# A new order of all operations for attention and a mixture of experts on one core, with one more head group masked on TensorE

## The chip, the core and the metric

The kernel runs on one core of a Trainium2 chip. The metric is device microseconds of one execution, the median of the runs shown: 206.53 us (206.17 to 207.06). Five engines work side by side, each through its own instruction stream in order: TensorE (PE: matrix products, with its weight loads as PEld), VectorE (DVE), ScalarE (ACT), GpSimd (POOL) and SyncE (SP). They meet through semaphores. POOL issues nearly all DMAs here, so a wait in its stream holds back the loads behind it.

## The reference

```python
# q, k, v: (8 batches, 8 heads, 576, 64)
scores = scale * q @ k.T                       # per batch and head
scores = where(|i - j| <= 32, scores, -1e9)    # a band of 65 keys
attn = softmax(scores)                         # over the keys
x = (attn @ v) as 4608 tokens of 512
logits = x @ w_gate + modality_bias[modality_id]
e = argmax(logits); gate = softmax(logits)[e]
out = gate * (relu(x @ w1[e]) @ w2[e])         # the one expert of each token
```

With the data of this problem the modality decides the expert, so two of the eight experts are used. A flag at the end of the kernel checks that and would start a general version otherwise.

## The kernel before

The whole program is one text, `ORDER` (L34 on): a list of operations, each with its indices, the engine that runs it (`/v` DVE, `/a` ACT, `/p` POOL, none for TensorE) and the PSUM banks it writes (`:0123`). A loop at the end of the kernel walks the list and emits each operation. Nothing is reordered afterwards: the order of the list is the order in each engine's stream, and semaphores make an operation wait for what it reads and for the banks or buffers it overwrites.

Operations of attention, for batch b, head group g (four heads) and head pair it (four a batch):

- `l b.u.g` and `lv b.i` (L222, L246): loads of q, k and of halves of v, issued by POOL.
- `t b.g.u` (L645): a DVE transpose of q or k. `SA`, `SB` (L677, for b below 3) and `SA`, `SE` (L701): the scores, in banks of PSUM. `sa`, `sb`, `se` (L685, L688, L733, L744): the exponentials, on ACT, into `pt`.
- The band's mask is put on in one of two ways. For the head groups numbered in `PM` (number 2b + g), `MA` and `MB` (L654, L658) first write 0 or a large negative number into the PSUM banks by products of an identity with the tile `neg`, and the scores are added on top. For the other groups `M it` (L766; `M b.g` L758, `Me` L752 from batch 3 on) multiplies the exponentials by 0 or 1 on DVE.
- `V it` (L804, L781): the products with v, whose extra column gives the softmax sums. `v it` (L818, L833): reciprocal and scaling on DVE, into `xt`. `Vx` copies v shifted by 64 rows.

Operations of the sorting and the experts:

- `s` and `G` rank the tokens of each modality and make one-hot matrices; `X b.m` (L853) moves and transposes a block of tokens by a product with one, and `pa`, `pb` (L873, L887, ACT) append it at the front or the back of the list `XT`. `Jo`, `Je`, `Jm`, `Jx`, `Jy` make the row numbers for the scatter of the output.
- `W` (L635, L637): loads of the weights of the two experts; each needs the expert's number in a POOL register, which DVE makes in `e4`.
- `U t.i` (L991): eight products of 128x256, a quarter of the hidden layer of token tile t; `u` (L1006 on DVE, L1008 on ACT) is its relu. `D t.s.h` (L1017): four products of 128x512, half of an output block; `y` (L1033 on DVE, L1031 on ACT) scales it by the gate and `O` (L1040) scatters it to the output. `L`, `lo`, `E`, `sm`, `rc` make the gates.
- `n k.256` (L1049): k products of zeros on TensorE, 128x256, that nobody reads.

Of the kernel before, what the change touches and what calls it, by code (L numbers as in the profile page):

```python
# [39 lines left out]
Kb/v Kc2/p sb0.1/a n2.256:4 MA0.1:4567 t1.0.1/v l1.1.1/p SA0.1 Kc0/p sa0.1/a s1:0 l1.0.1/p V0:12 s2/v s3/v  # L40
n2.256:3 W1.0/p s5 v0/v s4 s6/a s7 SB1.0:4567 s9/a s8/v s10/a s11/v G0/v V1:01 s12/p W1.1/p n2.256:2 s13/v
n2.256:2 sb1.0/a v1/v V2:23 lv1.1/p v2/v V3:01 r0/a Kc4/p v3/v SA1.0:4567 n2.256:3 W2.0/p s15/v sa1.0/a X0.1:0
t1.1.0/v n4.256:1 Kc5/p n2.256:2 n2.256:1 X0.0:1 s14/v l2.0.2/p t1.1.1/v n4.256:6 pa0.0/a pb0.0/a n4.256:3
# [16 lines left out]
D3.1.1 L2:1 se3.2/a lo2/v U5.2:2 SA3.1.0:4567 SA3.1.1 t4.1.1/v SA3.1.2 t4.0.1/v Kx0/a y3.0/a Vx3.0/v G3/v  # L60
U4.1:1 sa3.1/a U4.0:0 u5.2/a SE4.2.0:4567 u4.0/a SE4.2.1 se4.2/a Me3.2/v y3.1/v l5.0.2/p U5.0:2 O1.0/p l5.1.2/p
lv4.1/p E2/a u5.0/a u4.1/a U5.1:0 u5.1/a V12:45 sm2/v V13:67 M3.1/v v13/v O2.0/p U4.2:2 V14:01 U4.3:3 v14/v
c1/v u4.2/a u4.3/a v12/v V15:67 Vx4.1/a v15/v U5.3:0 D4.0.0:3 lv5.0/p D4.0.1 rc2/v lv5.1/p Me4.2/v O1.1/p
y4.0/v l6.1.2/p u5.3/a X3.0:6 pa3.0/a pb3.0/a lv6.0/p X3.1:7 X3.2:4 pa3.1/a O3.0/p D5.0.0:5 pb3.1/a t5.1.1/v
# [25 lines left out]
U14.2:3 L8:7 U17.3:1 U15.3:2 u14.2/a D14.1.0:3 u17.0/a u14.3/v y13.0/v E7/a U15.1:6 D14.0.0:5 U17.1:4 u17.1/a  # L90
O11.1/p O13.0/p D14.1.1 O10.1/p u15.3/v sm7/v E9/a rc7/v y12.1/v u17.3/v D14.0.1 U16.0:1 O11.0/p U15.2:4
u15.2/v sm9/v U16.3:0 U15.0:2 D17.0.0:4 O12.0/p u15.1/a y14.1/a O12.1/p rc9/v lo8/v D17.1.0:7 D17.1.1 U16.2:3
D17.0.1 Jy12/v E8/a sm8/v rc8/v y17.1/a c5/v c6/v O17.1/p O14.1/p y14.0/a u16.0/a u16.3/a c7/v O14.0/p U18.0:5
u18.0/a c9/v c10/v c11/v c8/v c12/v c13/v c14:1 c15/v U16.1:7 u16.2/a c16/v y17.0/v O17.0/p D18.0.0:5 U18.1:4
# [1228 lines left out]
```

## Time and profile before

| | |
|---|---|
| median of 3 runs | 206.53 us |
| the profiled execution | 206.92 us, its span 205.2 us |
| busy PE, DVE, ACT, POOL | 192.2, 151.2, 127.8, 92.8 us |
| products of zeros | 86, listed busy 13.9 us |
| granted TensorE clock over the span | 0.992 |

The profile is one execution. Its span runs from the first to the last instruction, and 1.7 us of the execution's time lie around it. The ends of products on TensorE are modelled: each is drawn about 0.17 us longer than its share of the array, so that gaps shorter than that don't show, and the price of a group of products is better read from where the next group starts.

### The profile page before, as it was taken

What the parts mean: (1) busy time and instruction counts of PE and PEld (TensorE: products, weight loads), DVE (VectorE), ACT (ScalarE), POOL (GpSimd) and SP (SyncE); (2) the same over time, 40 slices, a digit from 0 to 9 for tenths busy, and PEclk for the clock granted to TensorE, in tenths of its full rate; (3) what the DMA queues carried; (4) which work ended last, traced back from release to release, by engine and by line L of the source; (5) the groups of instructions that cost most, each with busy time, mean ns of one, the idle gap of its engine ahead of it and who ended that gap; (6) DMA issues with size and microseconds to landing.
All of it is one profiled execution on the core that took longest, in us unless ns stands there. A gap on an engine that the chain in (4) does not pass through costs nothing. (4 is left out here: it accounts for less than half of the span.)

```text
span 205.2 us, 6637 instructions
## 1 busy us (share of the span) xinstructions
PE 192.2 (94%) x2783; PEld 138.6 (68%) x2783; DVE 151.2 (74%) x314; ACT 127.8 (62%) x219; POOL 92.8 (45%) x137
## 2 busy tenths in 40 slices
...
PEclk9999999999999999999999999999999999999996
...
GB/s 66 205 177 182 212 213 191 213 213 192 204 188 234 217 234 194 218 213 64 184 161 153 147 262 150 188 195 13 3 56 2 0 107 0 205 54 74 161 131 55
DMA packets 47662, 30.43 MB, mean 148 GB/s; under 512 B 38883, under 2 KB 38923, under 8 KB 47371
## 3 DMA queue, kind: packets, MB, share of 16 engines
...
q8 instruction: 23, 0.38, 0.7%
...
HBM read 36.76 MB, written 9.70 MB: 226 GB/s over the span
## 5 line engine op out<-in xcount | busy, mean ns | idle before, releaser
L1040 POOL DMA_INDIRECT out_dram<-ys,ids x37 | 38.1, 1029 | 75.1 <-ACT ys L1031 33.5
L991 PE MATMUL banks<-XT,w_sb 128*128 128x256 bf16 x576 | 70.8, 273 | 0.6 <-DVE xt L833 0.3
L1017 PE MATMUL banks<-w_sb,hT 128*128 128x512 bf16 x288 | 69.2, 379 | 0.1
L991 PEld LDWEIGHTS <-w_sb 128*128 128x128 bf16 x576 | 54.0, 98 | 10.3 <-issue 1.3
L1008 ACT ACTIVATE hT<-banks 128x512 bf16<-128x512 f32 x53 | 30.1, 604 | 28.1 <-PE banks L991 24.5
L1017 PEld LDWEIGHTS <-hT 128*128 128x128 bf16 x296 | 27.3, 98 | 25.7
L645 DVE STREAM_TRANSPOSE qk<-qk 128x576 int32<-128x576 int32 x32 | 37.9, 1238 | 2.0 <-DMA qk<-in_k_dram 1.5
L833 DVE TENSOR_TENSOR xt<-banks,recs 128x640 bf16<-128x640 f32 x32 | 26.4, 824 | 1.1
L1006 DVE TENSOR_SCALAR hT<-banks 128x512 bf16<-128x512 f32 x21 | 14.4, 684 | 17.1 <-PE banks L991 17.1
L1031 ACT ACTIVATE ys<-banks,Gt 128x512 f32<-128x512 f32 x21 | 14.3, 691 | 15.0 <-PE banks L1017 9.6
L873 ACT CAST XT<-banks 128x352 f32 (+3 forms) x40 | 17.8, 446 | 6.2 <-PE banks L853 5.6
L246 POOL DMA_DIRECT2D vt<-in_v_dram x16 | 20.2, 1267 | 1.4 <-PE banks L781 1.3
L685 ACT ACTIVATE pt<-banks 128x1536 bf16<-128x1536 f32 x12 | 17.5, 1459 | 3.0 <-PE banks L677 2.0
L887 ACT CAST XT<-banks 128x352 f32 (+2 forms) x39 | 17.3, 444 | 1.2 <-DVE qk L645 0.5
L733 ACT ACTIVATE pt<-banks 128x1536 bf16<-128x1536 f32 x10 | 14.6, 1461 | 3.3 <-PE banks L701 3.3
L1033 DVE TENSOR_SCALAR ys<-banks,Gt 128x512 f32<-128x512 f32 x16 | 11.9, 745 | 5.9 <-PE banks L1017 5.9
L1049 PE MATMUL banks<-zero_b 128*128 128x256 bf16 x86 | 13.9, 319 | 2.0 <-DVE zero_b L303 1.5
L853 PEld LDWEIGHTS <-xt 128*128 128x128 bf16 x160 | 10.3, 98 | 4.3 <-issue 1.3
L781 PEld LDWEIGHTS <-pt 128*128 128x128 bf16 x320 | 11.7, 97 | 1.8 <-DVE pt L758 0.6
L853 PE MATMUL banks<-oh,xt 128*128 128x128 bf16 (+1 forms) x160 | 12.3, 214 | 0.7 <-DVE xt L833 0.3
L781 PE MATMUL banks<-vt,pt 128*128 128x65 bf16 x160 | 12.1, 193 | 0.4 <-DVE pt L758 0.4
L1049 PEld LDWEIGHTS <-zero_b 128*128 128x128 bf16 x86 | 9.3, 115 | 4.4 <-DVE zero_b L303 1.5
...
## 6 DMA issues: line engine op xcount, KB each, us to landing
...
out_dram<-ys,ids POOLq DMA_INDIRECT x37, 3.2
```

Source lines behind the costliest of these rows:

```text
L246: nc.gpsimd.dma_start(v_t[b % NV][:, n_ * i:n_ * i + n_, 0:D], v[b].rearrange("h s d -> (h s) d").rearrange("(n p) d -> p n d", p=P)[:, n_ ...
L645: nc.vector.transpose(qk_t[b % 2][:, g, at:at + S].rearrange("p (t r) -> p r t", r=R), Ct["l", b][:, u, g].bitcast(I32).rearrange("p (r j) ...
L685: nc.scalar.activation(pt[:, :, 2 * part:2 * part + 2, 0:WIN], st[:, :, 0:2 * WIN].rearrange("p h (j c) -> p h j c", c=WIN), ACT.Exp, scal ...
L781: nc.tensor.matmul(ot[:, h, (D + 1) * m:(D + 1) * (m + 1)], pt[:, c1:c1 + P], src[:, R // 2 * hp + n_, 0:D + 1], start=(i_ == 0), stop=las ...
L833: nc.vector.tensor_tensor(out=o_ap, in0=o_v[:, :, :, 0:D], in1=rec.unsqueeze(3).to_broadcast([P, 2, NM, D]), op=ALU.mult)
L853: nc.tensor.matmul(t_[:, kd, :], x_t[b % NX][:, m, P * kd:P * kd + P], Ct["oh", b][:, m, 0:n_], start=True, stop=True, skip_group_check=True)
L873: ins = nc.scalar.copy(XT[:, :, bass.ds(r_, w_)], Ct["X", b, m][:, :, 0:w_])
L991: ins = nc.tensor.matmul(ph[:, u_, :], w1[:, f0:f0 + 2 * P - 1:2], rhs, start=(kd == 0), stop=(kd == n_kd - 1))
L1008: nc.scalar.activation(o_ap, i_ap, ACT.Relu)
L1017: nc.tensor.matmul(Ct["D", t_, s_], Ct["h", t_][:, kf, P * s_:P * s_ + P], w2, start=(kf == 0), stop=(kf == n_kf - 1))
L1040: ins = nc.gpsimd.indirect_dma_start(out=out, out_offset=bass.IndirectOffsetOnAxis(ap=ids[:, u_:u_ + 1], axis=0), in_=Ct["y", t_, s_][:], ...
L1049: nc.tensor.matmul(banks[:, bk[0], 0:w_], zero_b[:, 0:P], zero_b[:, 0:w_], start=True, stop=True, skip_group_check=True)
```

## The change

The list is replaced as a whole, and `PM` gets a third number. So batch 1's first head group is masked by products: `MB1.0` and `MA1.0` are new and `M4`, `M5` are gone. The list keeps every other operation once. The products of zeros become 36 instead of 86; 21 of them stand ahead of the first real product, where 50 stood. Some operations change engine: 12 `u` from ACT to DVE and 10 the other way; 11 `y` from DVE to ACT and 7 the other way; three halves of `Vx` from ACT to DVE and one the other way; 6 `Je` from POOL to DVE and 5 the other way; the paddings `Kq0` and `Kp1` from DVE to ACT; `s10`, `s12`, `e9` to DVE.

```diff
-Km Kh/v Kw0/v Ke/v Ki l0.0.1/p n2.256:0 n2.256:0 l0.1.0/p Kp0/a n2.256:0 l0.0.0/p n4.256:0 Kg l0.1.1/p e0/v
...
-n2.256:0 n2.256:0 n2.256:0 n2.256:0 MA0.0:0123 Kw1/v Ko2/a Ko1/v t0.1.0/v lv1.0/p Ko0/a SA0.0 MB0.0:4567
-sa0.0/a t0.1.1/v Kc1/p SB0.0 lv0.1/p s0/v e4/v t1.0.0/v MB0.1:0123 sb0.0/a Kc3/p SB0.1 e5/v e7/v e8/v Kw2/v
...
-s16/p pa0.1/a X0.2:5 M5/v n2.256:4 pb0.1/a SB1.1:1234 l2.1.2/p pb0.2/a n4.256:0 G1/v pa0.2/a e9/p X0.3:7
-sb1.1/a V5:56 M4/v n2.256:0 n2.256:0 X0.4:0 v5/v pb0.3/a V4:12 pa0.3/a Jo0/v SA1.1:3456 pa0.4/a Je1.0/v pb0.4/a
-U0.1:7 v4/v sa1.1/a Je1.1/p U0.2:0 Je1.2/v Jo1/v r3/a L0:3 Je0.0/v Je0.1/v Je0.2/v U0.3:4 M6/v u0.1/a U1.0:6
...
+Km Kh/v Ki Kw0/v l0.0.0/p Kq0/a Kp0/a Kj/p Kn0/p t0.0.0/v l0.1.0/p l0.1.1/p Kq1/a Kp1/a t0.0.1/v e0/v e1/v Ke/v
+e2/v t0.1.1/v Kn1/p Kw1/v n4.256:4 n4.256:4 n4.256:4 n4.256:4 n5.256:4 MA0.0:0123 l0.0.1/p MB0.0:4567 SA0.0
+sa0.0/a l1.0.1/p Kc3/p Ko0/v e3/v t0.1.0/v l1.0.0/p s0/v SB0.0 MA0.1:0123 sb0.0/a l1.1.0/p lv0.0/p Kw2/v SA0.1
+s1:4 t1.1.0/v s2/v s11/v sa0.1/a n3.256:5 s4:4 Kc0/p s5:4 Kc2/p s3/v Kb/v n5.256:5 MB0.1:0123 t1.0.0/v t1.0.1/v
+s6/a l1.1.1/p s7:4 s8/v s10/v s9/a Ko1/a s12/v SB0.1 sb0.1/a Kc1/p G0/v e4/v n7.256:6 V0:45 s13/v lv0.1/p s15/v
+Kc4/p r0/a V1:67 MB1.0:0123 v0/v SB1.0 sb1.0/a V2:45 lv1.0/p t1.1.1/v v1/v W1.0/p V3:67 lv1.1/p SA1.1:0123
+s14/v v2/v v3/v G1/v SB1.1:4567 sa1.1/a sb1.1/a W1.1/p s16/p Jo1/v MA1.0:0123 SA1.0 Je0.0/v r3/a X0.4:4 Kc7/p
+Je1.0/v e6/v Jo0/v sa1.0/a Je1.1/v X0.1:5 X0.2:6 Kc5/p Je0.1/p Je0.2/p X0.0:7 pa0.0/a pa0.1/a pa0.2/a V4:01
+l2.0.2/p Je1.2/p pb0.0/a V5:23 pb0.1/a pb0.2/a M7/v M6/v X0.3:7 pa0.3/a pa0.4/a Jm0:5 v4/v Jx0/v V6:01 pb0.3/a
+v5/v Je2.0/v V7:56 U0.3:7 l2.1.2/p U0.0:2 Je2.1/p U0.2:3 v7/v v6/v W2.0/p pb0.4/a X1.1:0 X1.3:1 X1.0:5 pa1.0/a
...
+y16.0/a O12.1/p D17.1.0:4 u18.0/v y15.0/v D17.0.0:0 U18.1:2 c14:6 c15/v c16/v D17.0.1 y17.0/a O15.1/p
+O15.0/p O14.0/p rc9/v O16.0/p D17.1.1 O17.0/p y17.1/a O17.1/p D16.1.0:6 D16.1.1 y16.1/a D18.0.0:4 u18.1/v
+O16.1/p D18.0.1 y18.0/a O18.0/p c17/p
...
-    PM = (0,1)
+    PM = (0,1,2)
```

## Rows read from the trace of the kernel before

**Rows 1.** The page: busy time of TensorE and the granted clock in 40 slices.

```profile
PE 192.2 (94%) x2783; PEld 138.6 (68%) x2783; DVE 151.2 (74%) x314; ACT 127.8 (62%) x219; POOL 92.8 (45%) x137
...
PEclk9999999999999999999999999999999999999996
```

**Rows 2.** Stages: from and to in us, their length, busy us of each engine.

```profile
9.80:29.70 19.90, 17.52 (x354) 13.51 (x352) 18.70 (x41) 16.20 (x26) 15.74 (x32) 1.00 1.52 195
29.70:60.00 30.30, 29.81 (x412) 22.77 (x409) 29.02 (x67) 23.13 (x40) 14.97 (x23) 1.00 1.37 202
60.00:90.00 30.00, 29.14 (x537) 20.30 (x535) 29.21 (x44) 24.86 (x46) 16.51 (x16) 1.00 1.70 217
90.00:115.00 25.00, 24.56 (x440) 18.67 (x439) 22.93 (x38) 16.81 (x26) 11.37 (x14) 1.00 0.78 147
...
135.00:198.00 63.00, 62.95 (x688) 43.23 (x685) 29.73 (x74) 27.75 (x54) 17.00 (x18) 1.00 0.19 69
```

**Rows 3.** Timeline of the end: start, duration, engine, line, tiles, count, idle before.

```profile
192.60 5.34 PE L1017 MATMUL banks<-w_sb,hT 128*128 128x512 bf16 x24
...
198.03 0.69 ACT L1031 ACTIVATE ys<-banks,Gt 128x512 f32<-128x512 f32 x1 [1.90 <-PE banks L1017]
199.00 0.97 POOL L1040 DMA_INDIRECT out_dram<-ys,ids  x1 [0.34 <-ACT ys L1031]
```

**Rows 4.** Waits of TensorE after 29.7 us: the longest; total us, times, longest.

```profile
PE banks L781 <- DVE pt L758: 0.4, 1, 0.4
```

**Rows 5.** Timeline of TensorE, 12 to 40 us.

```profile
12.63 0.81 PE L654 MATMUL banks<-neg,ident 128*128 128x384 bf16 x4
13.28 0.39 PE L658 MATMUL banks<-neg,ident 128*128 128x128 bf16 x4
13.60 0.64 PE L677 MATMUL banks<-qk 32*128 32x192 bf16 x24
...
16.61 0.73 PE L804 MATMUL banks<-vt,pt 128*128 128x65 bf16 x18
17.17 0.38 PE L1049 MATMUL banks<-zero_b 128*128 128x256 bf16 x2
...
29.71 1.91 PE L991 MATMUL banks<-XT,w_sb 128*128 128x256 bf16 x16
31.46 0.55 PE L918 MATMUL banks<-wgd,XT 128*128 128x8 bf16 x16
...
39.47 0.49 PE L527 MATMUL banks<-ev,vx 128*128 128x72 bf16 x10
```

**Rows 6.** Timeline of DVE, 7 to 27 us.

```profile
7.21 1.26 DVE L645 STREAM_TRANSPOSE qk<-qk 128x576 int32<-128x576 int32 x1 [1.52 <-DMA qk<-in_k_dram]
8.95 1.26 DVE L645 STREAM_TRANSPOSE qk<-qk 128x576 int32<-128x576 int32 x1 [0.48 <-DMA qk<-in_q_dram]
...
10.19 2.28 DVE L645 STREAM_TRANSPOSE qk<-qk 128x576 int32<-128x576 int32 x2
...
25.13 1.14 DVE L766 TENSOR_TENSOR pt<-pt,mask 128x1920 bf16<-128x1920 bf16 x1
26.20 0.86 DVE L497 TENSOR_TENSOR oh<-iob,col 128x640 bf16<-128x640 bf16 x1
```

**Rows 7.** Timeline of ACT, 11 to 27 us.

```profile
11.13 3.00 ACT L685 ACTIVATE pt<-banks 128x1536 bf16<-128x1536 f32 x2 [0.45 <-PE banks L677]
...
25.35 0.98 ACT L887 CAST XT<-banks 128x352 f32 x2
26.23 0.47 ACT L873 CAST XT<-banks 128x352 f32 x1
```

**Rows 8.** Timeline of POOL: the first weights' load is issued.

```profile
17.68 0.77 POOL L635 DMA_DIRECT2D w_sb<-in_moe_w_dram  x1 [0.71 <-issue]
```

**Rows 9.** Two stretches of the products of zeros alone: busy us and count.

```profile
1.50:7.30 5.80, 5.78 (x28) 4.12 (x29) 1.00 0.83 138
7.40:9.70 2.30, 2.30 (x24) 2.05 (x21) 1.00 1.18 197
```

More of the change, by code (lines that the diff above doesn't have):

```diff
@@ L40 @@
[L40 to L43, printed above, removed]
-s16/p pa0.1/a X0.2:5 M5/v n2.256:4 pb0.1/a SB1.1:1234 l2.1.2/p pb0.2/a n4.256:0 G1/v pa0.2/a e9/p X0.3:7
@@ L60 @@
[L60 to L64, printed above, removed]
@@ L90 @@
[L90 to L94, printed above, removed]
@@ new lines @@
+t2.0.0/v u0.1/a L1:7 t2.0.1/v SB2.0:0123 Je4.1/p sb2.0/a Je5.0/v s17/v e5/v Jo5/v L0:6 lo1/v U2.0:4 Jo4/v
+Je4.2/v U2.2:7 lo0/v u1.1/a Je5.1/p u2.2/a Je5.2/v Jm2:6 SA2.0:0123 t2.1.0/v t2.1.1/v sa2.0/a u2.0/a E0/a
+Je6.0/v Jo7/v D0.0.0:5 M9/v sm0/v M8/v D0.0.1 rc0/v SA2.1:0123 sa2.1/a D0.1.0:4 Jo6/v E1/a D2.0.0:7 Jy10/v
+Jx2/v t3.0.1/v y0.0/a SB2.1:0123 sb2.1/a e10/v Je6.1/p l4.1.2/p Je7.0/v sm1/v D0.1.1 U3.1:6 y0.1/a Je6.2/v
+D2.0.1 V8:01 u3.1/a V9:34 rc1/v Jy1/v lv3.1/p Je7.1/p U3.0:6 Je7.2/p M10/v u3.0/a M11/v Kr0/a Jm3:2 v8/v U3.3:5
@@ new lines @@
+y2.0/a D2.1.0:0 r1/a v9/v Kx0/a u3.3/a V11:34 t3.0.0/v U3.2:7 v11/v u3.2/a Jx3/v lv3.0/p V10:56 Kx1/a v10/v
+t3.1.0/v t3.1.1/v Jy3/v Jy0/v SA3.0.0:1234 SA3.0.1 SA3.0.2 sa3.0/a Jy4/v Jy5/v D2.1.1 X2.1:5 X2.0:6 Jy11/v
+D1.1.0:7 D1.1.1 G3/v Jy6/v pb2.0/a pa2.0/a Jy7/v y2.1/a SE3.2.0:0123 SE3.2.1 l4.0.2/p pa2.1/a pb2.1/a se3.2/a
+y1.1/v D3.1.0:6 X2.3:5 X2.2:4 pa2.2/a D3.1.1 D3.0.0:7 t4.1.1/v Me3.2/v Jy8/v Jy9/v O0.0/p Kr1/v y3.1/a X2.4:0
+M3.0/v D1.0.0:6 pb2.2/a SA3.1.0:1234 SA3.1.1 SA3.1.2 pa2.3/a pa2.4/a D1.0.1 pb2.3/a t4.0.1/v U4.0:5 pb2.4/a
@@ new lines @@
+u4.0/v L2:0 sa3.1/a M3.1/v l5.0.2/p Kc6/p O2.0/p lo2/v O0.1/p Vx3.0/a U5.1:1 Vx3.1/v s19/v t4.1.0/v t4.0.0/v
+c0/v D3.0.1 U5.0:0 V12:45 u5.0/a u5.1/a V13:23 O2.1/p U5.2:0 u5.2/a U4.1:1 u4.1/a v12/v U4.3:0 y1.0/a v13/v
+V14:45 v14/v U4.2:1 E2/a sm2/v y3.0/a V15:67 u4.3/v SE4.2.0:2345 SE4.2.1 u4.2/a t5.0.0/v se4.2/a D4.0.0:1
+D4.0.1 rc2/v y4.0/a v15/v SA4.1.0:2345 SA4.1.1 SA4.1.2 sa4.1/a lv4.1/p D5.0.0:0 lv4.0/p Me4.2/v X3.0:1 pa3.0/a
+Vx4.0/v t5.1.0/v Vx4.1/v lv5.0/p pb3.0/a O3.1/p O1.1/p l5.1.2/p X3.1:6 D4.1.0:7 lv6.1/p D4.1.1 r2/a pa3.1/a
@@ new lines @@
+U5.3:1 SA4.0.0:2345 y4.1/a pb3.1/a lv5.1/p u5.3/a SA4.0.1 SA4.0.2 O1.0/p M4.1/v l6.0.2/p sa4.0/a X3.3:6
+D5.1.0:7 D5.0.1 X3.2:2 pb3.2/a Kv/p pa3.2/a pb3.3/a V19:34 pa3.3/a M4.0/v lv6.0/p O4.0/p v19/v X3.4:5 pb3.4/a
+pa3.4/a D5.1.1 y5.1/v V18:12 V16:34 v16/v V17:56 U7.0:7 u7.0/a L3:3 y5.0/a t5.0.1/v v17/v U6.1:4 U7.2:7 u7.2/a
+U7.1:5 t5.1.1/v v18/v lo3/v t6.1.0/v G4/v u7.1/a U6.3:7 u6.3/a Vx5.0/v u6.1/a U6.0:5 E3/a SE5.2.0:0123 SE5.2.1
+se5.2/a s18/v U6.2:4 X4.0:7 U7.3:6 u7.3/a u6.2/v SA5.0.0:0123 SA5.0.1 pb4.0/a pa4.0/a SA5.0.2 D7.0.0:4 D7.0.1
@@ new lines @@
+X4.1:7 l6.1.2/p Jy12/v sa5.0/a u6.0/v t6.0.0/v l7.1.2/p X4.2:5 D6.1.0:6 pb4.1/a pb4.2/a sm3/v pa4.1/a D6.1.1
+pa4.2/a SA5.1.0:0123 SA5.1.1 t6.0.1/v M5.0/v rc3/v SA5.1.2 Me5.2/v D7.1.0:5 sa5.1/a O3.0/p D7.1.1 V20:01 y7.0/a
+e11/v V21:23 v21/v v20/v X4.3:4 pb4.3/a D6.0.0:7 D6.0.1 y6.1/a O4.1/p U9.2:6 pa4.3/a M5.1/v L4:0 lo4/v
+SA6.0.0:1234 l7.0.2/p O7.0/p SA6.0.1 SA6.0.2 y7.1/v sa6.0/a Vx6.0/v lv7.1/p U8.2:0 u9.2/v E4/a U9.0:5 sm4/v
+O5.1/p Vx5.1/v U9.1:1 u9.0/a y6.0/a O7.1/p U8.3:5 u8.3/a U8.0:7 u8.2/a u9.1/v O6.0/p O5.0/p V22:56 V23:01
@@ new lines @@
+u8.0/a t6.1.1/v D9.1.0:7 v22/v v23/v G5/v U9.3:5 u9.3/a X4.4:6 SE6.2.0:0123 SE6.2.1 pb4.4/a rc4/v U8.1:4 D9.1.1
+se6.2/a X5.4:5 pa4.4/a t7.0.1/v M6.0/v SA6.1.0:0123 u8.1/a y9.1/v SA6.1.1 SA6.1.2 sa6.1/a X5.1:6 X5.0:4
+D9.0.0:7 D9.0.1 Me6.2/v X5.2:0 c1/v O6.1/p pa5.0/a lv7.0/p D8.1.0:1 pa5.1/a X5.3:2 M6.1/v pa5.2/a pb5.0/a
+pa5.3/a pa5.4/a t7.1.1/v G6/v D8.1.1 pb5.1/a y8.1/a O8.1/p Vx6.1/v U10.2:4 pb5.2/a t7.1.0/v pb5.3/a pb5.4/a
+U10.0:6 u10.0/a V24:01 V26:23 y9.0/a v24/v U11.1:6 u11.1/a V25:01 U11.0:7 v26/v t7.0.0/v c2/v L5:2 c3/v u11.0/a
@@ new lines @@
+U10.1:3 lo5/v v25/v O9.0/p U11.3:2 V27:67 U11.2:0 u11.2/a D11.1.0:1 u10.2/v v27/v X6.0:0 O9.1/p Vx7.1/v u10.1/a
+E5/a u11.3/v SA7.1.0:4567 sm5/v SA7.1.1 SA7.1.2 sa7.1/a G7/v U10.3:3 u10.3/v D10.0.0:2 pa6.0/a Vx7.0/v M7.1/v
+SE7.2.0:4567 SE7.2.1 D10.1.0:3 D10.0.1 rc5/v y10.0/v se7.2/a D11.1.1 y11.1/v pb6.0/a X6.1:0 SA7.0.0:4567
+SA7.0.1 SA7.0.2 sa7.0/a pb6.1/a D8.0.0:2 D8.0.1 pa6.1/a Me7.2/v X6.2:4 pb6.2/a V31:56 D11.0.0:0 D11.0.1 v31/v
+D10.1.1 y10.1/a V30:56 U13.0:7 pa6.2/a X6.3:4 O10.0/p U13.2:3 O10.1/p O11.1/p U12.3:1 v30/v c4/v M7.0/v y11.0/v
@@ new lines @@
+V28:56 pa6.3/a U13.3:0 v28/v u13.0/v u13.2/a U13.1:3 V29:56 y8.0/a O8.0/p U12.0:7 X6.4:2 u12.3/a v29/v U12.2:1
+u13.3/v e12/v u12.0/v pb6.3/a X7.0:5 pa6.4/a u13.1/v pb6.4/a pb7.0/a X7.1:2 L6:0 U12.1:7 lo6/v X7.3:0 X7.2:3
+pa7.0/a pa7.1/a pa7.2/a D13.1.0:5 u12.2/a u12.1/v D12.1.0:7 U14.0:1 X7.4:6 u14.0/v N/p D12.1.1 pb7.1/a pb7.2/a
+pa7.3/a U14.2:1 D13.0.0:3 E6/a sm6/v pb7.3/a pa7.4/a xe/a e13/v D13.0.1 D13.1.1 L7:6 lo7/v c5/v c6/v c7/v
+U15.1:0 L8:6 lo8/v L9:2 lo9/v c9/v c10/v E8/a U15.0:4 u15.0/a D12.0.0:2 U14.3:4 u14.2/a rc6/v u14.3/v U15.2:1
@@ new lines @@
+u15.1/a D15.0.0:0 U14.1:4 E7/a sm7/v u15.2/a y13.0/v sm8/v y13.1/v D12.0.1 U15.3:5 u15.3/a U16.3:1 D15.0.1
+U16.1:5 y12.1/a y12.0/a rc7/v O11.0/p u14.1/a D14.1.0:4 U16.0:2 u16.0/v rc8/v c11/v c8/v c12/v c13/v U16.2:7 Wx
+D14.1.1 D14.0.0:2 D15.1.0:3 y14.1/v O13.1/p O13.0/p D14.0.1 D15.1.1 y14.0/v U17.1:4 U17.3:2 U18.0:6 u16.1/a
+U17.0:5 u17.1/a U17.2:4 y15.1/a u17.3/v E9/a u17.2/v sm9/v D16.0.0:2 O12.0/p u16.2/a u17.0/a O14.1/p u16.3/a
+D16.0.1 y16.0/a O12.1/p D17.1.0:4 u18.0/v y15.0/v D17.0.0:0 U18.1:2 c14:6 c15/v c16/v D17.0.1 y17.0/a O15.1/p
```

45 lines of the change are left out of this document (3 added, 42 removed).

## The prediction, made before the changed kernel ran

> **What bounds the kernel now.** I read the page first. TensorE is busy for 192.2 of 205.2 us, and its granted clock is full in all slices but the last [rows 1]. The stages then say who is late where [rows 2]. From 9.80 to 29.70 TensorE is busy 17.52 of 19.90 us, and part of that is products of zeros, so here it waits for what DVE and ACT make. From 29.70 on it has nothing but real products and stands still for 0.49, 0.86 and 0.44 us in the next three stages, and 0.05 us in the 63 us from 135 on. So the second part is a fixed amount of products and less than 2 us of visible waiting. In the two stages up to 90 us DVE is busy 29.02 of 30.30 and 29.21 of 30.00 us: it is the other engine without slack, and the longest wait of TensorE there is for DVE's mask multiplication [rows 4]. The end of the timeline shows what follows TensorE: the last product ends at 192.60 + 5.34 = 197.94, ACT scales it by 198.72, POOL scatters it from 199.00, and the span ends at 205.2 [rows 3].
>
> So the time is: when the first expert product starts, plus the products still to do then, plus waits, plus a tail of 7.3 us. For each of the four I ask what the new list does.
>
> **The start, to the first expert product.** It stands at 29.71 now (U0.1) [rows 5]. In the new list the first is U0.3, and I follow its chain.
>
> On POOL, q of group 0 is now first, then the identity, one band of `neg`, and then k. The second and third load of the list before release their transposes at 7.21 and 8.95, 1.74 us apart [rows 6]; that is the pace of the loads, and k, now second, should still land near 7.2, with q transposed while it is awaited. One more transpose is 2.28 / 2 = 1.14 us [rows 6]. I take SA0.0 at 8.6, where the list before starts its first exponential at 11.13 [rows 7], so ACT starts near 9.1. The mask products MA0.0 and MB0.0 stand ahead of it, beside the loads, and cost nothing.
>
> A large exponential is 3.00 / 2 = 1.5 us at most [rows 7]. sa0.0 and sb0.0 fill ACT to 12.3. The fourth load and its transpose are no earlier than before (10.19 + 2.28 = 12.47 there [rows 6]), so sa0.1 runs 13.0 to 14.5. MB0.1 is written into the same banks 0 to 3 and waits for that. MA and MB cost 13.28 - 12.63 = 0.65 us, and 0.32 more for the third part of MB [rows 5], so MB0.1 is 0.97; s7 and SB0.1 follow, and sb0.1 ends near 18.0. MB1.0 needs its banks again: 0.97 and about 0.6 for the scores bring sb1.0 to 19.7 - 21.5. V2, V3 and SA1.1 follow, sa1.1 to 23.9. SB1.1 takes banks 4 to 7 and so waits for v3 on DVE, which I put at 23.4 by the list; sb1.1 to 26.0, sa1.0 to 27.4. Then eight appends of (26.23 - 25.35) / 2 = 0.44 us [rows 7], the last of which frees bank 7: U0.3 at 31.1. M7, M6 and v4 on DVE end at 29.7 by the same count, so V6 and V7 fit in before it.
>
> That is 1.4 us later than now. But V6 and V7 are done by then, where the list before does them after its first U: a V is 17.17 - 16.61 = 0.56 us, two are 1.12, and Jm0 is under 0.49 (I take 0.3) [rows 5]. What is left on TensorE is 1.4 us less. The start comes out even. The new masks are 2 x 0.65 + 0.32 = 1.62 us of TensorE [rows 5], all ahead of U0.3, where it has room; if ACT and DVE were faster than I count they would be on the path and cost the whole 1.62.
>
> **The products of zeros.** 50 fewer; those behind 9.8 us stand in front of real work only where TensorE waits anyhow. I take nothing for them; at most they free 36 x 2.30 / 24 = 3.5 us minus the new list's 15 x 0.1 = 1.5, so 2 us [rows 9].
>
> **DVE.** M4 and M5 go: 26.20 - 25.13 = 1.07 each [rows 6], 2.14 us. I compared both lists at V15, ahead of which both have the same real products but for SE4.2. DVE gets there two u more, six small Je for three, s10, s12 and e9, and loses half a Vx. Together these give back about 1.4, so 0.7 us less work. The paddings that moved to ACT lay in DVE's idle time and bring nothing. Also, DVE now waits less between 12 and 17 us, since a transpose stands where it waited for the rank products (about 1 us by the list's order). So DVE is 0.7 to 2 us ahead of the list before in the stages up to 90 us, where TensorE waits for it.
>
> **The waits after the first U.** 0.49 + 0.86 + 0.44 = 1.8 us are visible [rows 2]. Each wait hides up to 0.17 us more under the modelled end, so with some ten of them the sum is 3.3 at the most. Two of the three stages are those where DVE is full. I take half, 1.5 us. The bounds are 3.3 gained, and below nothing a new wait: an operation of the new list that stands before what it needs. The price of such a wait is at least the 0.4 us of rows 4.
>
> **The end.** The last product is now D18.0.1, with y18.0 on ACT and one scatter behind it. y, scatter and landing are as before: 198.03 to 198.72 and 0.28 to the scatter [rows 3]. No change, 0.3 us to either side.
>
> **The sum.** Start 0, masks 0, waits -1.5, end 0. The profiled execution took 206.92, so 205.4; it is 0.4 above the median of the runs, so 205.0.
>
> **The rivals.** *DVE still sets the pace and the waits return in other places.* For it: DVE is full to 97%, and 0.7 us of work is little. Against it: the operations that TensorE needs stand earlier in DVE's list relative to the products. It gives 206.5, no change.
>
> *TensorE drops to the lower clock in the start.* Here the change speaks against itself. The products of zeros show both levels: up to 7.3 us they follow each other every 5.80 / 28 = 0.21 us, which is 256 columns at 1.2 GHz, and then every 2.30 / 24 = 0.1 us, 2.4 GHz [rows 9]. The list before keeps TensorE busy 17.52 of 19.90 us from there; by my chain the new one leaves it idle for half of that stretch, in gaps of 1 us and more. If the clock falls between 10 and 31 us, then MB0.1, SB0.1, MB1.0, SB1.0, SB1.1, four X and two V on my chain, some 5 us together, take twice as long, less what waits hide: 4 us later, 209. It decides as soon as the granted clock shows one slice of 0.5 after 8 us. Against it: the gaps are short. The Trainium skill ("TensorE: Matmul & The Clock Gate", Part 1) has the lower rate as the array's default and the full one as something that activity earns; by that rule fewer idle products are a risk and by the trace, where the clock never fell after 7.3 us, no case shows how much is enough.
>
> *The first weights come late.* W1.0 needs the register from e4. It is issued at 17.68 now and U0.1 starts at 29.71, so it lands within 12.0 us [rows 5, 8]. The new list has e4 behind G0, near 18.1 by my count, so the load is issued at 18.8 and is there by 30.8, just ahead of U0.3. If DVE is 2 us late at e4 (three transposes, Kb and G0 stand ahead of it), U0.3 starts at 33 and everything behind it moves: 206.5 - 1.5 + 1.9 = 206.9, and with W1.1 and W2.0 as late in the same queue 208. For it: all loads go through one queue in order. Against it: the bound of 12.0 us is an upper one.
>
> That the mask isn't moved is no rival: `PM` and the list agree, and the two multiplications are gone.
>
> **Chances.** The forecast 0.52 (203.0 to 205.5 in itself), DVE and no change 0.27, the clock 0.12, the weights 0.09. About 0.5% (1.0 us) is what a measurement of this kernel can tell from no change. The forecast lies below 205.5, the second within; of the last two nearly all lies above 207.6, some of the weights' case within. So faster 0.53, same 0.28, slower 0.19. Unknown costs move the forecast by -3.3 + 1.5 = -1.8 at the waits and by -1 or +1.9 at the start. The range is 202.7 to 207.8; the clock's case and a part of the weights' stay outside.
>
> **What would show it.** Right: first exponential near 9.1, U0.3 between 30.5 and 32, M4 and M5 absent, TensorE's visible idle time from the first U to 115 us under 1 us, DVE busy less in the same stages. Wrong: idle TensorE of more than 2 us behind the first U (DVE or ACT named as releaser), a clock row below full after 8 us, or U0.3 behind 33 with a DMA as what ended the wait. The step I trust least is the chain to 31.1: it has nine links, and each is a bank or an engine that I counted by hand.

## The result and the profile after

The changed kernel takes 209.32 us (median of 16 runs, 208.19 to 211.49), the kernel before 207.04 (16 runs, 206.17 to 207.91): 1.0116 times as long, 95% interval 1.0092 to 1.0139. It is 1.2% slower; 205.0 was forecast. Ratios and intervals leave out executions that took over 1.5% longer than the fastest of the same kernel; medians count all.

The profiled executions took 210.18 and 206.92 us, 3.26 apart. Where they part can be read from three places. The first U starts at 33.66 instead of 29.71 [rows 5]; V6, V7 and Jm0 are done by then (1.4 us of products), so TensorE is 2.5 us behind there. Its last product ends at 198.48 + 1.89 = 200.37 instead of 197.94 [rows 3], 2.43 behind: from the first U to there it takes 166.71 instead of 168.23 us, and 1.4 of the difference are the products done earlier, so what lies between has gained 0.1. From there to the end of the execution it is 9.81 instead of 8.98 us, 0.83 more. So the start loses 2.5 us and the middle gains next to nothing of the 1.5 us that were forecast; whether the 0.8 at the end is the change's, the section on the end asks. (Line numbers of the changed kernels are one to four lower than before.)

The page of the changed kernel, TensorE's busy time and granted clock, against rows 1:

```profile
PE 189.0 (91%) x2745; PEld 135.7 (65%) x2745; DVE 148.3 (71%) x314; ACT 127.2 (61%) x221; POOL 94.7 (45%) x133
...
PEclk9969999999999999999999999999999999999996
```

One slice of the clock is at 6. The stages, against rows 2 (from and to, length, busy time of each engine, granted clock):

```profile
9.80:29.70 19.90, 15.06 (x291) 10.86 (x291) 19.19 (x53) 13.38 (x15) 14.63 (x32) 0.91 1.52 173
29.70:60.00 30.30, 29.37 (x449) 23.30 (x450) 29.29 (x65) 24.46 (x49) 17.29 (x19) 1.00 1.33 204
60.00:90.00 30.00, 30.00 (x533) 20.39 (x529) 25.85 (x50) 24.50 (x39) 17.60 (x18) 1.00 1.36 181
90.00:115.00 25.00, 22.66 (x409) 16.61 (x411) 20.71 (x37) 15.16 (x27) 10.90 (x14) 1.00 1.26 193
```

From 60 to 90 us the forecast holds: TensorE never waits (30.00 of 30.00, 29.14 before) and DVE is busy 25.85 us instead of 29.21. But from 90 to 115 TensorE is busy 22.66 of 25.00 us, 24.56 before: 1.9 us go there, more than the stage before gained.

The start on TensorE, DVE and ACT (timelines of the changed kernel: start, duration, engine, line, tiles; in brackets the idle time ahead and what ended it), against rows 5, 6 and 7:

```profile
5.98 2.12 PE L652 MATMUL banks<-neg,ident 128*128 128x384 bf16 x8
7.93 0.39 PE L656 MATMUL banks<-neg,ident 128*128 128x128 bf16 x4
10.64 1.66 PE L675 MATMUL banks<-qk 32*128 32x192 bf16 x40 [2.32 <-DVE pm__133 L589]
12.99 1.35 PE L652 MATMUL banks<-neg,ident 128*128 128x384 bf16 x4 [0.69 <-ACT pt L683]
...
33.66 2.56 PE L989 MATMUL banks<-XT,w_sb 128*128 128x256 bf16 x22
```

```profile
5.80 1.26 DVE L643 STREAM_TRANSPOSE qk<-qk 128x576 int32<-128x576 int32 x1 [4.34 <-DMA qk<-in_q_dram]
9.32 1.26 DVE L643 STREAM_TRANSPOSE qk<-qk 128x576 int32<-128x576 int32 x1 [2.26 <-DMA qk<-in_k_dram]
...
16.30 2.33 DVE L643 STREAM_TRANSPOSE qk<-qk 128x576 int32<-128x576 int32 x2
18.48 0.19 DVE L469 TENSOR_TENSOR col<-banks,Cw 128x40 bf16<-128x40 f32 x1
18.55 0.17 DVE L174 COPY off_f<-banks 128x41 f32<-128x41 f32 x1
```

```profile
11.49 2.79 ACT L683 ACTIVATE pt<-banks 128x1536 bf16<-128x1536 f32 x2 [5.14 <-PE banks L675]
...
18.75 0.19 ACT L172 CAST off_i<-banks 128x40 int32<-128x40 f32 x1 [2.31 <-DVE off_f L174]
...
19.00 1.46 ACT L683 ACTIVATE pt<-banks 128x1536 bf16<-128x1536 f32 x1
...
22.70 1.45 ACT L683 ACTIVATE pt<-banks 128x1536 bf16<-128x1536 f32 x1 [1.76 <-PE banks L675]
```

The reader is to see three things. The transpose of k runs at 9.32, not at 7.2, and SA0.0 at 10.64. ACT stands still for 2.31 us ahead of `s9`, which follows `s10`; `s10` has moved to DVE, behind two transposes (2.33 us together), and sb0.1 (19.00) is behind `s9`. Then ACT waits 1.76 us for MB1.0 and SB1.0. From 22.70 on it has exponentials and appends with one gap of 0.7 us up to the first U.

The wait of the middle, in the list of TensorE's waits (total, times, longest) and on DVE and POOL:

```profile
PE banks L779 <- DVE pt L750: 1.7, 1, 1.7
```

```profile
87.02 1.54 DVE L174 COPY vx<-vt 64x1122 bf16<-64x1122 bf16 x2 [3.01 <-DMA vt<-in_v_dram]
88.57 1.25 DVE L643 STREAM_TRANSPOSE qk<-qk 128x576 int32<-128x576 int32 x1
89.84 0.91 DVE L174 COPY vx<-vt 64x1122 bf16<-64x1122 bf16 x2
90.78 1.83 DVE L750 TENSOR_TENSOR pt<-pt,mask 128x1536 bf16<-128x1536 bf16 x2
```

```profile
70.42 1.29 POOL L1038 DMA_INDIRECT out_dram<-ys,ids  x1 [10.95 <-ACT XT L885]
...
77.00 0.97 POOL L1038 DMA_INDIRECT out_dram<-ys,ids  x1 [0.30 <-issue]
77.97 3.78 POOL L244 DMA_DIRECT2D vt<-in_v_dram  x3
```

The profile names DVE's mask (M4.1, M4.0) as what V19 waits for. DVE itself stands still for 3.0 us ahead of Vx4.1, for v of batch 4. POOL issues that load at 77.97, behind four scatters of the output, and the first of them (O0.0) had waited 10.95 us in POOL's stream. In the kernel before, POOL issues the two halves at 63.05 and 69.55.

What O0.0 had waited for is probably not the append on ACT that the profile names. Its data, y0.0, were ready at 53.1. A scatter also needs the table of row numbers, `ids`, which `Jy9` fills by a copy on DVE. Here is that copy, first before, then after:

```profile
56.05 0.18 DVE L176 CAST ids<-idf 128x37 int32<-128x37 f32 x1
```

```profile
69.33 0.18 DVE L174 CAST ids<-idf 128x37 int32<-128x37 f32 x1
```

In both, O0.0 starts 0.9 us behind the end of the copy (57.15 and 70.42), and so it does in lv4 (70.24). The new list has DVE make the table 13.3 us later, and the load of v waits behind the scatter that needs it. No run moves the table alone, so this link is read from the traces and not tested.

The end, against rows 3:

```profile
198.48 1.89 PE L1015 MATMUL banks<-wx,hT 128*128 128x512 bf16 x8
```

```profile
193.64 0.97 POOL L1038 DMA_INDIRECT out_dram<-ys,ids  x1 [3.03 <-DVE ys L1031]
...
201.37 0.97 POOL L1038 DMA_INDIRECT out_dram<-ys,ids  x1 [0.36 <-ACT ys L1029]
```

From 193.64 on, seven scatters follow each other at about 1.28 us. The last starts 1.00 us behind the last product, as before (1.06); the span ends at 208.5, 7.1 us behind it, where it was 6.2 before.

### The profile page after: what moved, and what is told of

Same layout as the page of the kernel before. It is cut to its first block, busy times and chain, and to the rows that moved or that the text cites. A ratio compares the mean times of both kernels' runs of the same rounds, so it can differ in the third digit from the quotient of the medians.

```text
span 208.5 us, 6539 instructions
## 1 busy us (share of the span) xinstructions
PE 189.0 (91%) x2745; PEld 135.7 (65%) x2745; DVE 148.3 (71%) x314; ACT 127.2 (61%) x221; POOL 94.7 (45%) x133
## 4 chain that ended last, share of the span: by engine, by line
PE 46%; DVE 15%; issue 12%; POOL 11%; DMA 8%; ACT 4%; ACTq 1%; POOLq 0%; DVEq 0%
PE banks L1015 17%; PE banks L989 16%; POOL out_dram L1038 6%; DMA vt<-in_v_dram 5%; DVE qk L643 4%; PE banks L851 3%; DMA qk<-in_k_dram 3%; PE banks L779 2%; PE banks L699 2%; DVE pt L764 2%; DVE xt L831 2%; POOL vt L244 2%; DVE vx L495 1%; PE banks L802 1%; ACT hT L1006 1%
## 5 line engine op out<-in xcount | busy, mean ns | idle before, releaser
L1006 ACT ACTIVATE hT<-banks 128x512 bf16<-128x512 f32 x51 | 29.2, 601 | 29.6 <-PE banks L989 29.6
L643 DVE STREAM_TRANSPOSE qk<-qk 128x576 int32<-128x576 int32 x32 | 38.9, 1244 | 7.5 <-DMA qk<-in_q_dram 5.2
L1004 DVE TENSOR_SCALAR hT<-banks 128x512 bf16<-128x512 f32 x23 | 15.6, 685 | 15.0 <-PE banks L989 14.9
L1029 ACT ACTIVATE ys<-banks,Gt 128x512 f32<-128x512 f32 x25 | 17.1, 689 | 9.9 <-PE banks L1015 9.2
L816 DVE RECIPROCAL recs<-banks 128x10 f32<-128x10 f32 x32 | 6.6, 207 | 9.2 <-PE banks L779 8.8
L779 PE MATMUL banks<-vx,pt 128*128 128x65 bf16 x160 | 11.6, 193 | 1.7 <-DVE pt L750 1.7
L779 PE MATMUL banks<-vt,pt 128*128 128x65 bf16 x160 | 11.5, 193 | 0.0
L174 DVE COPY vx<-vt 64x1122 bf16<-64x1122 bf16 x18 | 8.8, 488 | 3.3 <-DMA vt<-in_v_dram 3.0
```

What stands on the lines that cost most here:

```text
L643: nc.vector.transpose(qk_t[b % 2][:, g, at:at + S].rearrange("p (t r) -> p r t", r=R), Ct["l", b][:, u, g].bitcast(I32).rearrange("p (r j) ...
L779: nc.tensor.matmul(ot[:, h, (D + 1) * m:(D + 1) * (m + 1)], pt[:, c1:c1 + P], src[:, R // 2 * hp + n_, 0:D + 1], start=(i_ == 0), stop=las ...
L1006: nc.scalar.activation(o_ap, i_ap, ACT.Relu)
```

## The experiments

The first four kernels (lv4, warm, loads, both) ran on the first chip, where the kernel before takes 207.0 us. The others ran on two chips where it takes 218.2 to 219.6. All ratios are to the kernel before, timed beside them on the same chip, with 95% intervals. The expectations that are in us reckon from the first chip.

**The middle: lv4.** The two loads of v of batch 4 go ahead of O0.0.

```diff
-... Jy8/v Jy9/v O0.0/p ... sa4.1/a lv4.1/p D5.0.0:0 lv4.0/p Me4.2/v
+... Jy8/v Jy9/v lv4.0/p lv4.1/p O0.0/p ... sa4.1/a D5.0.0:0 Me4.2/v
```

> The changed list with the two loads of v of batch 4 moved ahead of O0.0 on POOL (nothing else). Theory 'DVE held by v': the copies Vx4.0 and Vx4.1 find their v, DVE isn't held for 3.0 us at 87.0, and TensorE's wait of 1.9 us ahead of V19 near 90 us goes; 1.2 to 1.9 us less than the changed kernel, 207.4 to 208.1. Rival 'other limit': V19 then waits for the next late thing (M4.0's scores or t5.x on DVE) and at most 0.5 us comes back. Rival 'start only': the loss is the start's, and the time after 60 us is a fixed amount of products anyway: no change within 0.4 us.

206.92 us, ratio 0.9988 (0.9964 to 1.0011): the whole net loss is gone, 2.4 us. The stage in its trace, the copies Vx4.1 and Vx4.0, now without a wait, and the first U and the last product:

```profile
90.00:115.00 25.00, 24.97 (x453) 18.65 (x451) 21.04 (x38) 16.56 (x29) 9.19 (x10) 1.00 1.24 188
```

```profile
84.40 1.35 DVE L172 COPY vx<-vt 64x1122 bf16<-64x1122 bf16 x2
...
87.04 0.91 DVE L172 COPY vx<-vt 64x1122 bf16<-64x1122 bf16 x2
```

```profile
33.48 2.78 PE L987 MATMUL banks<-XT,w_sb 128*128 128x256 bf16 x24
...
196.66 1.89 PE L1013 MATMUL banks<-wx,hT 128*128 128x512 bf16 x8
```

TensorE is busy 2.3 us more in the stage. So the 1.7 us that the profile put down to the mask were a load queued behind scatters. The first U is as late as in the changed kernel, but from there to the end of the last product (198.55) it is 165.07 us, where the kernel before takes 168.23. Less the 1.4 us of products done earlier, the middle gains 1.8 us: the gain that the prediction put at 1.5 is there as soon as the late load is gone, and it pays for most of the late start.

**The start: the clock (warm), late k (loads), both.** `warm` has 25 more products of zeros ahead of MA0.0, `loads` the four loads of batch 0 first, `both` the loads and 15 more zeros.

```diff
-Km Kh/v Ki Kw0/v l0.0.0/p Kq0/a Kp0/a Kj/p Kn0/p t0.0.0/v l0.1.0/p l0.1.1/p ... MA0.0:0123 l0.0.1/p
+Km Kh/v Ki Kw0/v l0.0.0/p l0.1.0/p l0.1.1/p l0.0.1/p Kq0/a Kp0/a Kj/p Kn0/p t0.0.0/v ... MA0.0:0123
```

> The changed list with 25 more products of zeros ahead of MA0.0, so that TensorE has no gap of 2.5 us ahead of SA0.0 (they add about 1.3 us at the slow rate and 19 x 0.1 us after it, so MA0.0 and MB0.0 end near 10.3 instead of 8.3). Theory 'clock': the granted clock stays at 1.00 from 10.7 to 14.1, MA0.1 takes 0.65 us instead of 1.28 to the next start, SA0.0 0.3 us less, and the first U starts about 0.9 us earlier than 33.6; median 208.4 instead of 209.3 (0.5 to 1.2 us less). Rival 'late k': the half clock lies beside waits for DVE's transposes, the clock row becomes full but the first U stays within 0.3 us of 33.6 and the time within 0.4 us of the changed kernel.

209.09 us, 1.0080 (1.0044 to 1.0116), not to be told from the changed kernel (1.0092 to 1.0139), though the intervals leave room for a part of the loss. The trace is of an execution of 207.45 us, one of three of eight below 208. The clock stayed full (0.51 in the changed kernel, 1.00 here), and the first U still starts at 33.48. Stage of the changed kernel, then of warm, and warm's ACT:

```profile
10.70:14.15 3.45, 2.76 (x44) 1.83 (x44) 3.42 (x18) 2.66 (x2) 2.87 (x10) 0.51 1.06 182
```

```profile
10.70:14.15 3.45, 1.85 (x42) 1.09 (x31) 3.08 (x8) 3.45 (x4) 2.87 (x10) 1.00 1.08 178
```

```profile
18.57 0.19 ACT L171 CAST off_i<-banks 128x40 int32<-128x40 f32 x1 [3.06 <-DVE off_f L173]
...
18.80 1.45 ACT L682 ACTIVATE pt<-banks 128x1536 bf16<-128x1536 f32 x1
```

TensorE had SB0.1's scores ready at 17.3, and ACT waited on for `s10`. What the clock gave to the first U, that wait took.

> The changed list with the four loads of batch 0 issued first on POOL, ahead of the identity and the bands of neg. Theory 'late k': the transpose of k starts at 7.2 to 7.5 instead of 9.32, SA0.0 at 8.6 to 9.0 instead of 10.64, DVE's row of transposes ends 1.5 to 2 us earlier, and the first U follows: 207.3 to 207.8, 1.5 to 2 us under the changed kernel. As TensorE's gap ahead of SA0.0 shrinks to some 0.5 us, the granted clock should stay full too, which adds up to 0.9 us. Rival 'clock alone': SA0.0 comes earlier but sb0.1 still ends near 20.9, because DVE or ACT sets it, and the time is within 0.5 us of 209.3.

208.4 us, 1.0030 (1.0002 to 1.0057): 0.9 us less by the medians, 1.8 by the ratios, whose intervals don't meet. SA0.0 starts at 8.63, where the prediction's chain had 8.6, and the first U at 32.57, 1.1 us earlier and still 1.5 behind the prediction's. In between V0 waits 0.49 and V2 0.78 us for v of batch 0. The clock did not stay full: it fell later, granted 0.68 from 14.00 to 17.40, and the time is less all the same.

> The four loads first and 15 more products of zeros ahead of MA0.0. If the clock matters beyond the late k, this is 0.5 us or more below the run with the loads alone; if the loads alone already keep the clock full, the two agree within 0.3 us; if the zeros delay MA0.0 and SA0.0 (TensorE busy past 8.6), it is up to 0.5 us slower than the loads alone.

208.68 us, 1.0061 (1.0032 to 1.0090). The zeros hold up SA0.0, since TensorE is busy with them past 8.6 (SA0.0 at 9.99), and the clock falls here too (granted 0.55 from 14.00 to 17.40); whether they cost time the intervals don't tell.

**The mask: mask_only and unmask.** The first moves the mask alone in the list before, the second takes it back in lv4's list.

```diff
-SB1.0:4567 ... SA1.0:4567 ... M5/v ... M4/v
+MB1.0:4567 SB1.0 ... MA1.0:4567 SA1.0
```

> The list before with the mask alone moved: PM has the third number, MB1.0 and MA1.0 stand ahead of SB1.0 and SA1.0, M4 and M5 are gone, all else and all products of zeros stay. Theory 'mask is neutral': both mask products lie beside waits of TensorE (ACT is held for the banks anyway at 19.8), DVE loses 2.1 us of work in a stretch where TensorE waits for it, and the time is 206.0 to 207.2. Rival 'mask pays 1.6 us': the 1.6 us of products stand on TensorE's path to the first U and nothing comes back: 207.9 to 208.7. Rival 'DVE relief': 204.5 to 205.8.

1.0030 (0.9991 to 1.0070), and again (mask_again) 1.0025 (0.9988 to 1.0061). The first U comes 0.6 us later than with the mask on DVE (30.40, and 29.80 in old_start below, which has the old start on the same kind of chip). The time is 0.6 us longer by the ratios, with intervals from 0.3 us less to 1.5 us more: neither the 1.6 us nor a gain worth naming, and whether DVE gives anything back isn't shown.

> The same kernel as mask_only (list before, mask of head group 2 on TensorE). In the first look its first U came at 30.4 instead of 29.7 and its ratio was 1.003 (0.999 to 1.007). Theory 'the mask costs at the start and DVE gives most of it back': 1.000 to 1.004. Rival 'mask pays 1.6 us': 1.006 to 1.009. Rival 'DVE relief': below 0.998.

> The changed list with the early loads of v of batch 4 (run lv4, 206.9) and the mask of head group 2 back on DVE: MB1.0 and MA1.0 gone, M5 and M4 behind Je1.1. Theory 'MB1.0 on the chain': ACT waits 1.8 us at 20.7 for MB1.0 and SB1.0; without MB1.0 sb1.0 starts 0.97 us earlier and the first U at about 32.5 instead of 33.5: 205.9 to 206.3. Rival 'DVE full': the 2.1 us of M4 and M5 are on DVE's path to v4 to v7 and V5, TensorE waits for them, 207.5 to 209. Rival 'neutral': within 0.4 us of 206.9.

1.0148 (1.0088 to 1.0208), against 1.0005 of lv4 on that kind of chip. In the new order sa1.0 is the last exponential of batch 1, and M5 and M4 can only follow it; V4 waits for them:

```profile
32.03 2.14 PE L800 MATMUL banks<-vt,pt 128*128 128x65 bf16 x36 [2.05 <-DVE pt L762]
```

The first U comes at 36.30. So this order needs the mask on TensorE, at the price of MB1.0 on ACT's path.

**The old start before the new rest: old_start.** The list before through U0.0, then the changed order with lv4's loads, the mask on DVE.

```diff
+Km Kh/v ... U0.0:3 v7/v l3.1.2/p        (list before)
+Kc7/p Jx0/v X1.1:0 X1.3:1 X1.0:5 ...    (changed list, what is left)
```

> The list before up to U0.0 (U0.1, U0.2, U0.3, U1.0, U1.2, V6, V7 included), and from there the changed list's order with the early loads of v of batch 4; the mask of group 2 on DVE as before. Theory 'the start is what the change lost': the first U is at 29.7 again and the rest has 1.5 to 2 us less of waits than before, with 0.8 us more at the end: 205.2 to 206.2. Rival 'the gain in waits was bought by the late start' (TensorE waits less because DVE had more time): the waits come back and it is 206.5 to 207.5.

1.0061 (1.0020 to 1.0102): no gain over lv4 (1.0005). The first U is at 29.80 again, but then TensorE waits for DVE and ACT:

```profile
35.00:60.00 25.00, 21.81 (x311) 16.25 (x308) 22.89 (x48) 17.05 (x29) 14.93 (x22) 1.00 1.33 204
```

24.57 of 25.00 in lv4_again, on the same kind of chip. This fits the rival: the small waits that the new order lacks are in part bought by its late start. It doesn't show it, for the joint itself may cost something, as the two lists were not made for each other, and DVE has M4 and M5 to do here.

**Mending more of the start: chain and four.** Both put `s9` behind sb0.1, t1.0.1 behind e4, and drop five zeros; they differ in how early v of batch 0 is loaded (chain: lv0.0 right behind Kn1; four: lv0.0 ahead of l1.1.0, and the end mended as below).

```diff
-MB0.1:0123 t1.0.0/v t1.0.1/v ... s9/a ... SB0.1 sb0.1/a ... G0/v e4/v
+MB0.1:0123 t1.0.0/v ... SB0.1 sb0.1/a s9/a ... G0/v e4/v t1.0.1/v
```

> Run lv4 with the start mended: four loads of batch 0 first, v of batch 0 right behind the bands of neg (lv0.1 ahead of l1.1.0), s9 on ACT behind sb0.1 instead of ahead of it, t1.0.1 on DVE behind e4, and the five products of zeros ahead of MB0.1 gone. Theory 'ACT's chain of exponentials sets the first U': ACT stood still 3.1 us ahead of s9 and sb0.1; sb0.1 starts near 16.0 instead of 18.8, sb1.0 near 19.7, and the first U at 31 to 31.5 instead of 33.5; the time falls by about as much, 204.5 to 205.3. Rival 'something else is late next' (v of batch 0 by DMA, the first weights, DVE): first U at 32.5 as in the run loads, 205.8 to 206.3. Rival 'the start is given back': behind the first U TensorE waits for DVE, first U early but the time within 0.5 us of 206.9.

1.0101 (1.0040 to 1.0162). v ahead of the next q held up DVE, and the first U fell back to 36.07:

```profile
15.60 1.26 DVE L641 STREAM_TRANSPOSE qk<-qk 128x576 int32<-128x576 int32 x1 [3.41 <-DMA qk<-in_q_dram]
```

> three, and on top the rest of ACT's waits in the start: s9 behind sb0.1, t1.0.1 on DVE behind e4, lv0.0 ahead of l1.1.0, and the five products of zeros ahead of MB0.1 gone. Theory 'ACT's chain sets the first U': sb0.1 starts about 1 us earlier than in loads (16.0 to 16.5) and the first U near 31.7 instead of 32.6, so 0.5 to 0.9 us less than three. Rival 'v of batch 0 by DMA': V2 waits for lv0.1 near 22 as in loads, the first U stays at 32.3 to 32.7 and the time within 0.3 us of three. If TensorE falls to half clock ahead of MB0.1 again it is 0.5 us slower.

0.9917 (0.9881 to 0.9953), no better than `three` below. sb0.1 now starts 0.05 us behind SB0.1, at 17.38, so `s9` no longer holds it. But V0, in the bank that `s9` reads, waits for it instead, and the first U is at 33.42. Here the clock lay on the path: it was granted 0.50 from 14.00 to 17.40, and from the start of MB0.1 to the next group behind SB0.1 it takes 2.91 us, where the changed kernel's trace has 1.66 at full clock. In the trace of `three` the clock is full there, so the two differ in more than the order.

```profile
19.46 1.44 PE L800 MATMUL banks<-vt,pt 128*128 128x65 bf16 x36 [0.52 <-ACT off_i L170]
```

**The end, alone and with the rest: tail, tail_only, three, lv4_loads.** y15.0 stood on DVE behind u18.0, and behind it the scatters piled up.

```diff
-y14.0/v U17.1:4 ... O12.0/p ... O14.1/p ... O12.1/p D17.1.0:4 u18.0/v y15.0/v ... O15.1/p O15.0/p O14.0/p
+y14.0/v y15.0/v O12.0/p O12.1/p O14.1/p O14.0/p O15.0/p U17.1:4 ... y15.1/a O15.1/p ... D17.1.0:4 u18.0/v
```

> The same kernel as the run lv4 (the two loads of v of batch 4 ahead of O0.0), as the base for the other three on the same chip. Theory 'DVE held by v': the ratio to the kernel before is 0.999 again (0.995 to 1.003). Rival 'the first run was luck': the ratio is 1.008 or more, as for the changed kernel.

1.0005 (0.9971 to 1.0039).

> Run lv4 with the end mended: y15.0 right behind y14.0 on DVE (it stood behind u18.0, so that DVE made it some 20 us late) and O12, O14, O15 ahead in the same way, so that POOL doesn't issue seven scatters at 1.28 us each to the very end. Theory 'scatters pile up': the last scatter lands as soon as before (6.2 us from its issue to the end of the span, 7.0 in lv4), 0.5 to 0.8 us less than lv4. Rival 'the end is set by the last scatter alone': no change within 0.3 us.

0.9896 (0.9847 to 0.9946), on lv4's list. The last y on ACT and the last scatters (first of lv4_again, then of tail; their last products end at 207.98 and 207.79):

```profile
208.33 1.27 ACT L1027 ACTIVATE ys<-banks,Gt 128x512 f32<-128x512 f32 x2 [2.29 <-PE banks L1013]
```

```profile
209.29 0.97 POOL L1036 DMA_INDIRECT out_dram<-ys,ids  x1 [2.00 <-ACT ys L1027]
210.56 0.97 POOL L1036 DMA_INDIRECT out_dram<-ys,ids  x1 [0.30 <-POOLq L1286]
```

```profile
208.79 0.97 POOL L1036 DMA_INDIRECT out_dram<-ys,ids  x1 [0.75 <-issue]
```

So the last scatter starts 2.6 us behind the last product in lv4_again and 1.0 in tail. All seven traces of this end on these chips have 2.6, the five of the mended end 1.0, mask_only with the end of the list before 1.05. From the last scatter to the end of the span it is no shorter (6.5 and 6.3 us). A row of scatters isn't what holds the last one: POOL stands still for 2.00 us ahead of the last but one, for a y, and ACT makes its last two y together, behind the last product. Why it does so with this end, the traces don't tell.

On the first chip the traces have nothing of this. In all five of this end (the changed kernel, warm, loads, both, lv4) the last scatter starts 1.0 us behind the last product. Behind it they have 5.4 us (warm, both) to 7.1 (the changed kernel), where the kernel before has 6.2. So the 0.8 us more at the end lie within what the landing differs by from trace to trace, and aren't shown to be the change's there.

> The changed list with nothing but the end mended. Theory 'scatters pile up': 0.4 to 1.1% under the changed kernel (1.0116): 1.001 to 1.008; the last scatter is issued within 0.4 us of the last y and the span ends 6.2 to 6.5 us behind it, instead of 7.1. Rival 'the last scatter alone': 1.010 to 1.014.

0.9921 (0.9893 to 0.9949).

> lv4, loads and tail together. If the three causes are separate and add up (2.4, 0.9 and 0.6 us off the changed kernel), 1.5 us less than lv4 and 0.7 to 0.9% less than the kernel before. Rival 'the earlier start is waited away': TensorE waits longer for DVE behind the first U and it stays within 0.4 us of the run tail.

0.9882 (0.9837 to 0.9928), and again (three_again) 0.9868 (0.9820 to 0.9915).

> The changed list with the early loads of v of batch 4 and the four loads of batch 0 first, the end as in the changed list. Theory 'start counts': the first U is 1.0 to 1.2 us earlier than in lv4 and the ratio to the kernel before is 0.4 to 0.5% lower than lv4's (0.9988 and 1.0005): 0.994 to 0.997. Rival 'the earlier start is waited away': 0.998 to 1.002, with more waiting of TensorE between 75 and 135 us.

0.9958 (0.9915 to 1.0000). So on these chips the end is worth about 1% (tail against lv4_again). The earlier start brings 0.1 to 0.7% (three against tail, lv4_loads against lv4_again and lv4_third), which these intervals don't separate from nothing; on the first chip it was 0.9 us by the medians.

> The same kernel as the run three. If the parts add up, lv4_loads less the gain of the end: 0.988 to 0.993; if the earlier start is waited away, the same as lv4 with the end mended (run tail, 0.9896).

**Does the loss hold on the other chips? after_again and lv4_third.** The changed kernel and lv4, unchanged, side by side.

> The changed kernel itself, once more, to see what its ratio is where the kernel before takes 218 us. Theory 'the loss is the same there': 1.009 to 1.014, so that the end mended alone (0.9921) is worth 1.9% there. Rival 'where TensorE is held up for 8 us more, DVE and the loads of v catch up and the wait of V19 shrinks': 0.998 to 1.006, with less than 1 us of waiting ahead of V19.

0.9989 (0.9960 to 1.0019): there the changed kernel is as fast as the one before. lv4_third comes to 1.0027 (0.9987 to 1.0067), so the early loads bring nothing. The copy Vx4.1 in the trace of after_again has no wait for v (POOL had issued the load at 78.35, as late as on the first chip):

```profile
87.86 1.04 DVE L174 COPY vx<-vt 64x1122 bf16<-64x1122 bf16 x2
```

The trace is of an execution of 221.43 us, the longest of twelve; that of tail_only, with the same late load, has no wait at its copy either (89.53), but it too is of the longest execution of its kernel.

> The same kernel as lv4, in the same call as the changed kernel. Theory 'V19 is worth the loss anywhere': about 1% under the changed kernel. Rival 'V19 counts only where TensorE is not held up by its weight loads': within 0.4% of it.

## Why the prediction was wrong

It failed at the start and at the waits. By the profiles on the first chip the start lost 2.5 us where the sum has 0; the waits gained the 1.5 us that the sum has, but a new wait of 1.7 us took them away.

- **"The waits after the first U ... I take half, 1.5 us."** The gain itself was right in mechanism and size: from 60 to 90 us DVE had slack and TensorE's 0.86 us of waits went, and without the new wait the middle gains 1.8 us (lv4). What failed is the other bound. The prediction had named the type ("an operation of the new list that stands before what it needs") and priced it at 0.4 us or more, from the largest wait that rows 4 showed, and the sum has nothing for it. The new wait of 1.7 us came at 90, and lv4 shows that its removal is worth the net loss. The prediction compared DVE's list up to V15, and POOL's behind the start not at all: a load behind scatters whose row numbers come late is seen only by walking POOL's stream.
- **"k, now second, should still land near 7.2."** The prediction names the identity and the band of `neg` ahead of k in POOL's stream and gives them no time: k is issued at 3.75 instead of 2.20 and its transpose runs 2.1 us later. The link "SA0.0 at 8.6" was right as soon as the loads stood first (8.63).
- **"U0.3 at 31.1", the start even.** It came at 33.66. One us of that is the late k (loads). The chain left out that `s9` waits for `s10` on DVE, ahead of sb0.1; warm shows that wait with the clock full. It had MB1.0 in ACT's way, and also priced the masks at nothing; 0.65 + 0.32 us of the 1.76 at 22.70 are MB1.0's [rows 5].
- **"No change, 0.3 us to either side" at the end.** On the first chip nothing shows it wrong: the last scatter follows the last product as closely as before, and the 0.83 us more lie in a landing that differs by 1.8 us between traces of the same end. On the other chips it is wrong: there the last scatter starts 1.5 us later behind the last product than with the end of the list before, and with y15.0 and its scatters moved the kernel gains 0.7 to 1.1% (tail against lv4_again, and tail_only against after_again on the other of the two chips, each by intervals that don't meet).

The range fails too, as 209.32 lies above it, and its ends don't come out of the bounds named: 205.0 - 1.8 - 1 is 202.2 and not 202.7, and 205.0 + 1.9 is 206.9, or 208.4 if the 1.5 us are not gained, and not 207.8.

**The rivals.** The clock's condition came true: granted 0.51 from 10.70 to 14.15, after TensorE had stood still for 2.3 us. And the time came out where that rival had put it, at 209. That is a coincidence of the number. With the clock held full the first U hardly moves (33.48 in warm), and in lv4 the clock falls as in the changed kernel (granted 0.91 from 9.80 to 29.70 in both) and the loss is gone. The Trainium skill ("TensorE: Matmul & The Clock Gate", Part 1) has the full rate as something that activity earns; the trace agrees, with 0.51 after the 2.3 us without products. In the changed kernel the lower clock lay beside a wait, and warm, without it, gains nothing that shows; in `four` it lay on the path, at 1.25 us more from MB0.1 to SB0.1. The view of the granted clock has a limit that rows 9 show: it reads 1.00 in both stretches, though the products follow each other every 0.21 us in the first and every 0.1 us in the second. The first weights are no cause either: in the changed kernel's trace the first U follows V7 without a wait. "DVE still sets the pace" may be half right, by old_start: with the early start TensorE waits for DVE and ACT.

What stays open: how much of the 2.5 us at the start would come back as time if it were mended. `loads` gives 0.9 us by the medians on the first chip, on the other chips the gain isn't told from nothing, and old_start, which points to waits that the late start saves, is a weak witness. The version with all three repairs (`three`) beats both kernels on the chips where it ran, 0.987 and 0.988; on the first chip only two of its parts were tried, each alone (lv4 and loads).
